# Three changes of order in a gated Fourier and attention kernel: half of q earlier, the gate earlier, a first chunk in pieces

## The chip, the cores and the metric

The kernel runs on one core of a Trainium2 chip. The metric is the device time of one execution in microseconds (us). A core has TensorE (PE in the profile; its weight loads are PEld), VectorE (DVE), ScalarE (ACT), GpSimd (POOL) and SyncE (SP), which only issues transfers. Each engine works through its own list of instructions in order and waits on semaphores for the others. Transfers are issued mostly from SyncE's queue, some from POOL's, and are carried out by 16 DMA engines.

## The reference

For x of 2048 rows and 512 columns the output mixes two branches with one gate per row:

```python
g = _sigmoid((x * gate_w).sum(-1, keepdims=True))
# branch a: real part of a Fourier transform along both axes, as matrix products
a = einsum("bsd,ed->bse", x, dft_hid_re);  b = einsum("bsd,ed->bse", x, dft_hid_im)
y = einsum("ts,bse->bte", dft_seq_re, a) - einsum("ts,bse->bte", dft_seq_im, b)
# branch b: attention with 32 heads of width 16
q, k, v = split(x @ wqkv)                       # per head: 2048 x 16
p = softmax(einsum("bhqd,bhkd->bhqk", q, k) * Dh ** -0.5)
o = einsum("bhqk,bhkd->bhqd", p, v) @ wo
return g * y + (1 - g) * o
```

All of it is float32.

## The kernel before, in words

Nearly every float32 factor is cut into a rounded high part and a low part (`hi_lo`: ACT copies to the high part, DVE or POOL subtracts to get the low part), and a product is made of three matrix products: high times high, high times low, low times high (`mm3`).

*Stage 1, q and k (lines 132 to 199).* x (four blocks of 512 rows, each in four chunks of 128 columns) and the weights of q, k and v are loaded as raw tiles of 128 x 512 into `RAW` = 6 buffers. `add` puts a load on a list; `load_ahead` (L113) issues loads from the list as long as fewer than five loaded tiles are waiting; `split(n)` (L118) cuts the next n of them into parts and loads on. The list starts with chunk 0 of q's weights and of x, then chunk 1 of both, and so on. TensorE first does ten products with zeros (L161), then `split(8)` has cut the first four chunks, and the products of the first chunk come in the order: four times weights high with x high, four times weights low with x high, four times weights high with x low (L183); then the other chunks with `mm3` (L91 to L93). Results go out as high and low parts to `qk_d` in memory. For the last two blocks of x `gate_row` (L166) sums x times gate_w on DVE into a column of `z`.

*Stage 2, v (L358 to L365).* After `qs` and `ks` were cleared, v is made: four chains of 12 products (L362), then three times `four` (L333), which runs four chains in half-height products with some of the attention's row maxima in between.

*Stage 3, imaginary hidden transform (L375), then `run_plan(0)`, the gate (`gate`, L764 to L770: one exponential on ACT, four operations on 128 x 16 elements on DVE, giving `g`, `ng` and `omg`), and a `four` with the weights `wre` (L1046).* `g` is used from the first results of the sequence transform on, `ng` and `omg` later.

*Stage 4, the long stage.* Two heads make a pair p (0 to 15). A pair is 32 units: for each half of the queries (columns LOW, 0 to 1023, and HIGH) 16 key tiles. Per unit the scores are computed (`scores`, L788) from `ks[p % 2]` and `qs[p % 2]`, ACT takes the exponential (L789), and `pv` (L824) multiplies with v. Before that, `a_tile` (L248) computes scores the other way round, and DVE reduces them to row maxima (L250); these maxima, negated, become three extra rows of `qs`, so that the scores come out already reduced. The sequence transform of branch a runs through the same segments (L457).

A segment is written out as a pattern of slots:

```python
FULL = "s a s s a a s s a a s a s a a s |"
```

In each slot one product of the transform runs on one half of the rows of the array, and beside it on the other half a score (s) or a maximum (a) of one head: head 1 in even segments, head 0 in odd ones. At the bar come late work, the sums, `run_plan(valued)`, and then the value products of two units. So a segment takes two units, and eight scores and eight maxima of one head.

*What sets the order of the loads.* `at(u, f, ...)` puts a call into a plan; `run_plan(u)` makes all calls that are due by u + 1. For pair p, with u = 32(p - 1), `load_q(p, LOW)` is put at u - 14, the loads of `ks` in quarters at u - 16 (head 1) and u - 14 (head 0) and every four units after that, `load_q(p, HIGH)` at u - 2. `load_q` (L227) issues three transfers from `qk_d` (L220) and one of zeros (`clear`, L225) that empties the rows of the maxima. On SyncE's queue there are also the stores of `osum` (L842, a half pair's result, which wait for POOL's sum), the chunks of `w_seq` (`c_load`, L392, one for every 12 products of the transform), the loads and stores of the normalising blocks (`block`, L582 to L602), and the rows of maxima (`m_rows`, L271, half of them on POOL's queue). Pairs alternate between `qs[0]` and `qs[1]`, so the load for pair p overwrites columns that the scores of pair p - 2 read: LOW is read by units 32(p - 2) to 32(p - 2) + 15, that is up to u - 17.

Of the kernel before, what the change touches and what calls it, by code (L numbers as in the profile page):

```python
# [10 lines left out]
F32 = mybir.dt.float32  # L11
F32R = mybir.dt.float32r
AF = mybir.ActivationFunctionType
ALU = mybir.AluOpType
AX = mybir.AxisListType

P = 128
# [5 lines left out]
KT = D // P  # L23
# [3 lines left out]
RAW = 6  # L27
# [5 lines left out]
def mix_kernel(ctx: ExitStack, tc: tile.TileContext, xa_t, xa, wqkv, w_hid, w_seq, wo, gate_w, out):  # L33
# [5 lines left out]
    nc = tc.nc  # L39
# [26 lines left out]
    z = const.tile([P, NT], F32, name="z")  # L66
    g = const.tile([P, NT], F32, name="g")
    ng = const.tile([P, NT], F32, name="ng")
    omg = const.tile([P, NT], F32, name="omg")
# [5 lines left out]
    xab = [const.tile([P, 4, 2, D], F32R, name=f"xab{tb}", tag=f"xab{tb}") for tb in range(4)]  # L75
# [10 lines left out]
    def hi_lo(hi, lo, src, lo_eng=None):  # L86
        nc.scalar.copy(hi, src)
        (lo_eng or nc.vector).tensor_tensor(lo, src, hi.bitcast(F32), ALU.subtract)

    def mm3(ps, sh, sl, mh, ml, first, last):  # L90
        nc.tensor.matmul(ps, sh, mh, start=first, stop=False)  # L91
        nc.tensor.matmul(ps, sh, ml, start=False, stop=False)  # L92
        nc.tensor.matmul(ps, sl, mh, start=False, stop=last)  # L93
# [9 lines left out]
    todo, loaded = [], []  # L103

    def staged(src):
        raw = st1.tile([P, D], F32, name="raw", bufs=RAW)
        nc.sync.dma_start(raw, src)
        return raw

    def add(hi, lo, src, lo_eng, shape=None):  # L110
        todo.append((hi, lo, src, lo_eng, shape))

    def load_ahead():  # L113
        while todo and len(loaded) < RAW - 1:
            hi, lo, src, lo_eng, shape = todo.pop(0)
            loaded.append((hi, lo, staged(src), lo_eng, shape))

    def split(n):  # L118

        for _ in range(n):  # L120
            load_ahead()
            if loaded:
                hi, lo, raw, lo_eng, shape = loaded.pop(0)
                hi_lo(hi, lo, raw.rearrange("p (s t) -> p s t", s=4) if shape else raw, lo_eng)
            load_ahead()

    def add_x(tb, kt):
        x = xab[tb][:, :, :, kt * P:(kt + 1) * P]
        add(x[:, :, 0], x[:, :, 1], xa_t[tb, :, kt], nc.vector, True)


    with tc.tile_pool(name="qk", bufs=1, reuse_waits="tile") as pool:
        wh = pool.tile([P, 2, KT, D], F32R, name="wh")
        wl = pool.tile([P, 2, KT, D], F32R, name="wl")

        def mm_qk(ps, c, ct, tb, kt):
            cols = slice(ct * P, (ct + 1) * P)
            x = xab[tb][:, :, :, kt * P:(kt + 1) * P]
            mm3(ps, wh[:, c, kt, cols], wl[:, c, kt, cols], x[:, :, 0], x[:, :, 1], kt == 0, kt == KT - 1)

        def evac_qk(ps, c, ct, tb):
            hl = pool.tile([P, 2, D], F32R, name="hl", bufs=7)
            hi_lo(hl[:, 0], hl[:, 1], ps)
            nc.sync.dma_start(qk_d[c][:, ct * P:(ct + 1) * P, tb * 512:(tb + 1) * 512].rearrange("v p t -> p v t"),
                              hl.bitcast(F32))

        for kt in range(KT):
            add(wh[:, 0, kt], wl[:, 0, kt], wqkv[0, :, kt], nc.vector)
            add_x(0, kt)
        for kt in range(KT):  # L150
            add(wh[:, 1, kt], wl[:, 1, kt], wqkv[1, :, kt], nc.vector)
        for tb in range(1, 4):
            for kt in range(KT):
                add_x(tb, kt)
        for kt in range(KT):
            add(wv[0][kt], wv[1][kt], wqkv[2, :, kt], nc.gpsimd)
        for kt in range(KT):
            add(wch[:, kt], wcl[:, kt], w_hid[1, :, kt], nc.gpsimd)
        ps = turn_of("f")
        for _ in range(10):  # L160
            nc.tensor.matmul(ps, zero, zero.unsqueeze(1).broadcast_to([P, 4, P]), start=True, stop=True)  # L161
        split(8)

        xgs = {}

        def gate_row(s):  # L166

            xg = xgs.pop(s)
            nc.vector.scalar_tensor_tensor(xg, xg, 1.0, gwb, op0=ALU.mult, op1=ALU.mult, accum_out=z[:, s:s + 1])
            if s + 5 < NT:  # L170
                xgs[s + 5] = staged(xa[s + 5])

        for tb in range(4):
            if tb == 2:
                assert not todo and not loaded
                nc.sync.dma_start(gwb, gate_w.broadcast_to([P, D]))
                xgs.update({s: staged(xa[s]) for s in range(5)})
            for c in range(2):
                if tb == 0 and c == 0:
                    pss = [turn_of("f") for _ in range(4)]  # L180
                    for w, v in ((wh, 0), (wl, 0), (wh, 1)):
                        for ct in range(4):
                            nc.tensor.matmul(pss[ct], w[:, c, 0, ct * P:(ct + 1) * P], xab[tb][:, :, v, :P],  # L183
                                             start=w is wh and not v, stop=False)
                    for kt in range(1, KT):
                        for ct in range(4):
                            mm_qk(pss[ct], c, ct, tb, kt)
                    split(4)
                    for ct in range(4):
                        evac_qk(pss[ct], c, ct, tb)  # L190
                    continue
                for ct in range(4):
                    ps = turn_of("f")
                    for kt in range(KT):
                        mm_qk(ps, c, ct, tb, kt)
                    split(1 if ct % 2 and tb else 2)
                    evac_qk(ps, c, ct, tb)
                    if tb > 1:
                        gate_row(8 * (tb - 2) + 4 * c + ct)
# [32 lines left out]
    LOW, HIGH = slice(0, S // 2), slice(S // 2, S)  # L232
# [93 lines left out]
    def maxima():  # L326

        nonlocal a_next
        users = [a_tile(a_next, h) for h in range(2)]
        a_next += 1  # L330
        return users[1]

    def four(ss, wh, wl, done, between=None):  # L333

        ps = [turn_of("s") for _ in ss]
        seen = None
        for phase, pair in enumerate(((0, 1), (2, 3), (1, 0), (3, 2))):
            guard, seen = seen, None
            both = [row_products(ss[c], wh, wl) for c in pair]
            for j in range(12):  # L340
                for half, c in enumerate(pair):
                    st, mv = next(both[half])
                    r = slice(64 * half, 64 * half + 64)
                    i = nc.tensor.matmul(ps[c], st[r], mv[r], start=phase < 2 and j == 0, stop=phase > 1 and j == 11)  # L344
                    if phase > 1 and j == 0:
                        tc.add_manual_dep(
                            i.ins, guard.ins.name,
                            mybir.DependencyInfo(mybir.DependencyClass.Sync, mybir.DependencyReason.DATA))
                if j in (((2, 7), (1, 5, 10), (3, 8), (1, 5, 10))[phase] if not between else (2, 6, 10)):
                    user = between(phase, j) if between else maxima()  # L350
                    seen = seen or user
            if deferred:
                deferred.pop(0)()
            if phase > 1:
                for c in sorted(pair):
                    done(ss[c], ps[c])

    for s in range(4):  # L358
        ps = turn_of("s")
# [401 lines left out]
        x.products((0,))  # L761


    def gate():  # L764

        nc.scalar.activation(ng, z, AF.Exp, bias=0.0, scale=-1.0)
        nc.vector.tensor_scalar(ng, ng, 1.0, None, op0=ALU.add)
        nc.vector.reciprocal(g, ng)
        nc.vector.tensor_scalar(ng, g, -1.0, None, op0=ALU.mult)
        nc.vector.tensor_scalar(omg, g, -1.0, 1.0, op0=ALU.mult, op1=ALU.add)  # L770

    pts = {}

    def scores(u, qb, h, ps=None):
# [109 lines left out]
    def at(u, f, *args):  # L884
        plan.setdefault(u, []).append(partial(f, *args))

    for p in range(2, NP):
        u = 32 * (p - 1)
        at(u - 14, load_q, p, LOW)
        for kb in range(4):  # L890
            cols = slice(kb * 512, (kb + 1) * 512)
            if 2 < p < NP - 1:
                at(u - 16 + 4 * kb, load_rows, p, 1, cols, (1,))
                at(u - 14 + 4 * kb, load_rows, p, 1, cols, (0,))
            else:
                at(u - 14 + 4 * kb, load_rows, p, 1, cols)
        at(u - 2, load_q, p, HIGH)

    for hf in range(2):
        for ct in range(4):  # L900
            n = 3 if hf and ct == 3 else 4
# [119 lines left out]

    both_first = chain_of(proj(1, (0, 1, 2), one), proj(0, (0, 1, 2), one))
    run_plan(0)
    gate()

    first_y = []

# [76 lines left out]
```

## Time and profile before

| | us |
|---|---|
| median of 3 runs | 1681.37 |
| lowest and highest | 1680.41, 1682.21 |
| the profiled execution | 1678.57 |
| its span, first to last instruction | 1676.4 |
| TensorE busy in it | 1659.6 (99%) |
| VectorE busy | 1375.9 (82%) |
| ScalarE busy | 1252.2 (75%) |
| GpSimd busy | 753.5 (45%) |

The granted TensorE clock was 0.999 over the span. Lines of the profile are quoted below as they stand. A row of the timeline is: start, duration, engine, line, operation, out<-in, shapes, count, and in brackets the idle time of the engine before it with what ended it. A row of the waits is: who waited, for whom, microseconds in total, times, the longest. A row of the chain is: start, duration, what ran. "SPq" is SyncE's queue issuing a transfer. L12 is line 12 of the kernel.

### The profile page before, as it was taken

Reading aid. Unit: us, or ns where it says so; the run is one execution under the profiler, and the core shown is the slowest. Engines: PE = TensorE matmul, PEld = TensorE weight load, DVE = VectorE, ACT = ScalarE, POOL = GpSimd, SP = SyncE. Lnnn points to the kernel's source line nnn. Section 1 sums busy time; section 2 is a strip of 40 time slices with the busy share of each in tenths; the row PEclk is TensorE's granted clock in tenths of the full one; section 3 lists DMA queues with packets and bytes.
Section 4 is the critical chain, followed back from the end, with each engine's and each line's share of the span. In section 5 each row is a group of like instructions: output and inputs, shape, how many; then the busy total and the mean of one; then the engine's idle time right before and its main releaser. Section 6 shows DMA issues by size and latency. Waiting matters only on the chain.

```text
span 1676.4 us, 35226 instructions
## 1 busy us (share of the span) xinstructions
PE 1659.6 (99%) x13170; PEld 991.0 (59%) x13170; DVE 1375.9 (82%) x2283; ACT 1252.2 (75%) x2486; POOL 753.5 (45%) x813
## 2 busy tenths in 40 slices
PE   9999999999999999999999999999999999999998
PEld 7888866655555555555555555555555555555554
DVE  5469988888888888888888888888888888877775
ACT  5212288878777787777787777877778788799996
POOL 0124644445454455544454555555445565432331
PEclk9999999999999999999999999999999999999999
DMA  9944301112121224222127324222222234451014
GB/s 299 341 152 142 155 1 38 28 55 77 55 72 47 69 83 123 73 58 71 50 79 245 85 89 124 85 82 73 65 71 64 80 96 124 157 189 47 15 53 140
DMA packets 92481, 165.66 MB, mean 99 GB/s; under 512 B 23360, under 2 KB 24776, under 8 KB 91160
## 3 DMA queue, kind: packets, MB, share of 16 engines
q1 hardware_dynamic: 87672, 162.64, 31.3%
q8 instruction: 104, 1.70, 0.4%
q0 software_dynamic: 4352, 0.39, 0.2%
q14 instruction: 65, 0.53, 0.1%
q10 hardware_dynamic: 288, 0.39, 0.1%
HBM read 107.73 MB, written 54.52 MB: 97 GB/s over the span
## 4 chain that ended last, share of the span: by engine, by line
PE 97%; DMA 1%; DVE 1%; SPq 1%; ACT 0%; issue 0%; DVEq 0%; ACTq 0%
PE d L457 36%; PE t L824 27%; PE t L248 11%; PE t L788 10%; PE t L344 5%; PE t L92 2%; PE t L93 2%; PE t L91 2%; PE t L805 1%; PE t L457 1%; PE t L362 1%; PE d L248 0%; SPq L220 0%; DMA ks<-qk 0%; DVE mx L250 0%; DMA qs<-zero 0%
## 5 line engine op out<-in xcount | busy, mean ns | idle before, releaser
L250 DVE TENSOR_REDUCE mx<-t 128x1 f32<-128x512 f32 x2009 | 1251.7, 684 | 230.4 <-PE t L248 198.9
L789 ACT ACTIVATE pt<-t 128x512 f32<-128x512 f32 x2048 | 1034.8, 632 | 19.8 <-PE t L788 9.5
L788 PE MATMUL t<-qs,ks 64*128 64x512 f32 x2048 | 728.4, 409 | 0.2
L248 PE MATMUL t<-ks,qs 64*128 64x512 f32 x2009 | 674.1, 398 | 8.6 <-DMA qs<-zero 3.6
L457 PE MATMUL d<-xab,ch 64*128 64x512 f32 x2016 | 657.1, 400 | 0.0
L824 PE MATMUL t<-pt,vt 128*32 128x512 f32 x3968 | 477.1, 598 | 0.0
L457 PEld LDWEIGHTS d<-xab,ch 64*128 64x128 f32 x2016 | 359.2, 184 | 142.4 <-issue 97.3
L248 PEld LDWEIGHTS t<-ks,qs 64*128 64x128 f32 x2009 | 358.5, 184 | 85.4 <-ACT pt L789 50.5
L788 PEld LDWEIGHTS t<-qs,ks 64*128 64x128 f32 x2048 | 366.6, 184 | 69.6 <-DVE mx L250 40.0
L457 PE MATMUL d<-xab,cl 64*128 64x512 f32 x1008 | 404.0, 401 | 0.0
L839 POOL TENSOR_TENSOR osum<-osum,oe 128x512 f32<-128x512 f32 x217 | 279.5, 1288 | 157.9 <-ACT oe L833 155.3
L833 ACT COPY oe<-t 128x512 f32<-128x512 f32 x217 | 127.4, 587 | 214.8 <-PE t L824 213.1
L824 PEld LDWEIGHTS t<-pt,vt 128*32 128x32 f32 x3968 | 103.6, 109 | 232.1 <-issue 150.5
L402 POOL CAST ch<-craw 128x512 fp32r<-128x512 f32 x126 | 77.2, 613 | 359.6 <-PE t L788 290.3
L457 PEld LDWEIGHTS d<-xab,cl 64*128 64x128 f32 x1008 | 185.7, 184 | 72.7 <-issue 50.3
L403 POOL TENSOR_TENSOR cl<-craw,ch 128x512 fp32r<-128x512 f32 x126 | 162.3, 1288 | 10.2
L271 POOL DMA_DIRECT2D qs<-mt x132 | 73.6, 563 | 88.7 <-DVE mt L267 78.8
L457 PE MATMUL d<-wo_hl,o_hl 64*128 64x512 f32 x288 | 75.8, 395 | 0.0
L457 PE MATMUL d<-wre,xab 64*128 64x512 f32 x288 | 70.4, 389 | 0.0
L457 PEld LDWEIGHTS d<-wo_hl,o_hl 64*128 64x128 f32 x288 | 51.6, 184 | 18.3 <-ACT pt L789 13.4
L457 PEld LDWEIGHTS d<-wre,xab 64*128 64x128 f32 x288 | 52.8, 184 | 3.1
L92 PE MATMUL t<-xab,wh 128*128 128x512 f32 x124 | 48.3, 389 | 0.0
(118 smaller groups left out, 944.8 us busy)
## 6 DMA issues: line engine op xcount, KB each, us to landing
craw<-w_seq SPq DMA_DIRECT2D x128, 256.0 KB
qk<-hl SPq DMA_DIRECT2D x32, 512.0 KB
qs<-qk SPq DMA_DIRECT2D x84, 128.0 KB
ks<-qk SPq DMA_DIRECT2D x288, 32.0 KB
b<-hl SPq DMA_DIRECT2D x16, 512.0 KB
xab<-b SPq DMA_DIRECT2D x16, 512.0 KB
o<-osum SPq DMA_DIRECT2D x62, 128.0 KB
oh<-nh SPq DMA_DIRECT2D x12, 512.0 KB
```

The lines of the kernel that those rows point to most:

```text
L92: nc.tensor.matmul(ps, sh, ml, start=False, stop=False)
L248: nc.tensor.matmul(ps, qs[p % 2][r, qt * P:(qt + 1) * P], ks[p % 2][r, kb * 512:(kb + 1) * 512], start=True, stop=True)
L250: user = nc.vector.tensor_reduce(mx[p % 2][:, h, qt, kb:kb + 1], ps, AX.X, ALU.max)
L344: i = nc.tensor.matmul(ps[c], st[r], mv[r], start=phase < 2 and j == 0, stop=phase > 1 and j == 11)
L402: nc.gpsimd.tensor_copy(h1, raw)
L403: nc.gpsimd.tensor_tensor(l1, raw, h1.bitcast(F32), ALU.subtract)
L457: i = nc.tensor.matmul(self.ps, st[r], mv[r], start=not self.begun, stop=stop)
L788: nc.tensor.matmul(ps, ks[p % 2][rr, kt * P:(kt + 1) * P], qs[p % 2][rr, q0:q0 + 512], start=True, stop=True)
L789: return nc.scalar.activation(pts[u][:, 2 * qb + h], ps, AF.Exp, bias=0.0, scale=DH ** -0.5)
L824: nc.tensor.matmul(acc[32 * j:32 * j + 32], vt[:, kt, p, h:h + 32], pt[:, j], start=u == us[0], stop=u == us[-1])
L833: nc.scalar.copy(oe, acc)
L839: nc.gpsimd.tensor_tensor(o, o, oe, ALU.add)
```

## The change

Three things are moved. First, `load_q(p, LOW)` is planned at u - 18 in place of u - 14, for all pairs from 2 on. Second, the five operations of the gate stand ahead of the chains of v in place of behind `run_plan(0)`. Third, the first chunk: x is loaded first and its weights second, outside of the list; x's high part is made first on ACT; the high part of the weights is made in four pieces of 128 columns, alternately on DVE and ACT; then DVE makes the low part of the weights and that of x. Nine products with zeros are done in place of ten, and `split(6)` follows for the other three chunks. No arithmetic is added or left out beside the one product with zeros.

```diff
-    def load_ahead():
-        while todo and len(loaded) < RAW - 1:
+    def load_ahead(n=RAW - 1):
+        while todo and len(loaded) < n:
...
-        for kt in range(KT):
+        first = staged(xa_t[0, :, 0]), staged(wqkv[0, :, 0])
+        for kt in range(1, KT):
             add(wh[:, 0, kt], wl[:, 0, kt], wqkv[0, :, kt], nc.vector)
             add_x(0, kt)
...
-        for _ in range(10):
+        for _ in range(9):
             nc.tensor.matmul(ps, zero, zero.unsqueeze(1).broadcast_to([P, 4, P]), start=True, stop=True)
-        split(8)
+        load_ahead(RAW - 2)
+        x, raw = xab[0][:, :, :, :P], first[0].rearrange("p (s t) -> p s t", s=4)
+        nc.scalar.copy(x[:, :, 0], raw)
+        for ct in range(4):
+            cols = slice(ct * P, (ct + 1) * P)
+            (nc.scalar.copy if ct % 2 else nc.vector.tensor_copy)(wh[:, 0, 0, cols], first[1][:, cols])
+        nc.vector.tensor_tensor(wl[:, 0, 0], first[1], wh[:, 0, 0].bitcast(F32), ALU.subtract)
+        nc.vector.tensor_tensor(x[:, :, 1], raw, x[:, :, 0].bitcast(F32), ALU.subtract)
+        split(6)
...
+    nc.scalar.activation(ng, z, AF.Exp, bias=0.0, scale=-1.0)
+    nc.vector.tensor_scalar(ng, ng, 1.0, None, op0=ALU.add)
+    nc.vector.reciprocal(g, ng)
+    nc.vector.tensor_scalar(ng, g, -1.0, None, op0=ALU.mult)
+    nc.vector.tensor_scalar(omg, g, -1.0, 1.0, op0=ALU.mult, op1=ALU.add)
+
     for s in range(4):
         ps = turn_of("s")
...
-        at(u - 14, load_q, p, LOW)
+        at(u - 18, load_q, p, LOW)
...
     run_plan(0)
-    gate()
```

More of the change, by code (lines that the diff above doesn't have):

```diff
@@ L761, in last_pair @@
         x.products((0,))
[L764 to L770, printed above, removed]
     pts = {}
```

## The prediction

> **What bounds the kernel now.** I read the page first. The chain of work that ended last is almost all matrix products, so only time in which TensorE stands still, or is held to a slower pace, can be won or lost.
>
> ```profile
> PE 97%; DMA 1%; DVE 1%; SPq 1%; ACT 0%; issue 0%; DVEq 0%; ACTq 0%
> ```
>
> Next the view of waits for TensorE alone. Its idle time in the whole span is small, and nearly all of it stands in front of L248, the products of `a_tile`:
>
> ```profile
> PE t L248 <- DMA qs<-zero: 3.6, 2, 2.9
> PE t L248 <- DMA ks<-qk: 3.4, 2, 1.7
> PE t L248 <- ACT pt L789: 1.3, 2, 1.0
> ```
>
> Then the chain in order of time. Every group of value products (L824, 16 products) marks the end of one segment of the plan, so the distance between two groups is one segment. The list leaves some groups out; a distance of two segments is then split.
>
> ```profile
> 356.42 1.85 PE t L824 x16
> 362.73 1.85 PE t L824 x16
> 368.54 1.85 PE t L824 x16
> ...
> 449.89 1.85 PE t L824 x16
> ...
> 457.58 1.85 PE t L824 x16
> ...
> 544.68 1.85 PE t L824 x16
> 550.67 1.85 PE t L824 x16
> ...
> 631.92 1.86 PE t L824 x16
> 642.84 2.80 DMA qs<-zero
> ...
> 646.75 1.85 PE t L824 x16
> ...
> 733.82 1.85 PE t L824 x16
> ...
> 741.61 1.86 PE t L824 x16
> ...
> 916.05 1.85 PE t L824 x16
> ...
> 928.50 1.85 PE t L824 x16
> ...
> 1015.53 1.90 PE t L824 x16
> ...
> 1022.58 1.85 PE t L824 x16
> ```
>
> A regular segment takes 368.54 - 362.73 = 5.81 us. Once in each pair of heads a segment is longer. Pair 3: 362.73 - 356.42 = 6.31, an excess of 0.50. Pair 4: 7.69, excess 1.88. Pair 5: 5.99, excess 0.18. Pair 6: 646.75 - 631.92 = 14.83 for two, excess 3.21. Pair 7: 7.79, excess 1.98. Pair 9: 928.50 - 916.05 = 12.45 for two, excess 0.83. Pair 10: 7.05, excess 1.24. Together 9.82 us. It is always the segment that ends at unit u - 12 of its pair (u = 32(p - 1)), and by the pattern FULL its 14th slot of 16 holds the first `a_tile` of pair p, for head 1. That product is the first reader of the LOW columns of `qs`, which `load_q` writes at u - 14: three transfers of q and one of zeros.
>
> SyncE's queue shows why they are late (pair 6, then pairs 9 and 5):
>
> ```profile
> 627.83 0.38 SPq L392 DMA_DIRECT2D craw<-w_seq  x1
> ...
> 634.62 1.15 SPq L842 DMA_DIRECT2D o<-osum  x2
> ...
> 640.90 1.76 SPq L220 DMA_DIRECT2D qs<-qk  x3
> ```
>
> ```profile
> 920.64 1.78 SPq L220 DMA_DIRECT2D ks<-qk  x3
> ```
>
> ```profile
> 542.26 1.74 SPq L220 DMA_DIRECT2D qs<-qk  x3
> ```
>
> One issue takes about 0.6 us of the queue. In pair 6 the two stores of `osum` had waited, and the loads of `ks`, the four loads of a normalising block and a chunk of `w_seq` stood ahead of q. So q went out at 640.90 and the zeros at 642.84, the product began at 645.77 by the chain (642.84 + 2.80, and the wait's tail), 2.9 us late. In pair 5 q went out at 542.26, ahead of its segment (which begins with the group at 544.68), and the excess is only 0.18. I read the excess as lateness of q plus about 0.18 us that the first products on freshly written columns cost anyway.
>
> **The change part by part.**
>
> *First half of q four units sooner.* Nothing is added or removed: the same four issues go onto SyncE's queue two segments (11.6 us) earlier in program order, for pairs 2 to 15. In pair 6 that is after the load at 627.83, where the queue did little until the stores at 634.62. The four take 640.90 to 643.50 = 2.6 us there. What they are moved past: the stores of `osum`, three loads of `ks` for head 1 (u - 16), block loads and one or two chunk loads. Those now start up to 2.6 us later if the queue is full, and not at all later where it stood waiting for POOL's sum, as in pair 6. The loads of `ks` for head 0, behind q at u - 14, go 2.6 us sooner. What the moved loads must wait for: they overwrite columns that the scores of pair p - 2 read, units up to u - 17. FULL gives eight scores of one head to a segment, that is four units; by the plan at u - 18 head 1 has all of unit u - 17 from the segment before, and head 0 has reached u - 15. So the last reader runs in the first half of the segment that precedes the plan, and the queue does not stand long. Both q and zeros should then have landed some 5 us or more before the first reader.
>
> What is late next is `ks` of head 1. In pair 9 its issue ends at 920.64 + 1.78 = 922.42. In pair 6 the reader started 645.77 - 643.50 = 2.3 us after the last issue ended, so `ks` can be read at 924.7. The reader is due 5.1 us after its segment's first group (pair 6: 645.77 less the wait of 2.9 is 642.9, the group is at 631.92 + 5.81 = 637.7), in pair 9 at 916.05 + 5.81 + 5.1 = 927.0. That leaves 2.3 us, so the cover holds in the worst pair that I found.
>
> Worth: 9.82 us less seven times the 0.18 that pair 5 keeps, 9.82 - 1.26 = 8.6 us. Ends: 5 us if `ks` or a slow transfer takes back some of the places, 11 us if nothing at all remains and the pairs that I have not listed give another half microsecond each. I take 8.6, from the rows of pair 5.
>
> *The gate ahead of the v chains.* One exponential on ACT and four small operations on DVE move from the start of the stage with `wre` to the start of the v chains.
>
> ```profile
> 198.79 0.75 DVE L767 TENSOR_SCALAR ng<-ng 128x16 f32<-128x16 f32 x1 [0.24 <-ACT ng L766]
> ```
>
> ```profile
> 199.35 1.09 PE L344 MATMUL t<-wre,xab 64*128 64x512 f32 x8
> ...
> 200.82 1.41 PE L344 MATMUL t<-wre,xab 64*128 64x512 f32 x8
> ...
> 204.47 1.30 PE L344 MATMUL t<-wre,xab 64*128 64x512 f32 x8
> ...
> 205.61 1.29 PE L344 MATMUL t<-wre,xab 64*128 64x512 f32 x8
> ```
>
> Before, DVE is held by the gate between its maxima, and TensorE waits for the banks that those maxima free. Groups of eight products (with two products for maxima between them) come every 205.61 - 204.47 = 1.14 us; behind the gate the distance is 200.82 - 199.35 = 1.47, so 0.33 us too long. In the new place the work is covered: DVE has nothing there.
>
> ```profile
> 105.05 2.08 DVE L250 TENSOR_REDUCE mx<-t 128x1 f32<-128x512 f32 x3 [7.95 <-PE t L248]
> ```
>
> The added wait, ACT's for the last row of `z`, has the copies of `v` behind it, and these wait longer for other things; if the cover were gone the price would be the gate's own length, some 1.5 us. Ends: a gain of 1.5 us (all of the gate) and a loss of 1.5; I take a gain of 0.3, the rows' figure.
>
> *The first chunk.* x is loaded and copied first, the weights are copied in four pieces on DVE and ACT, and one of ten warming products goes.
>
> ```profile
> 1.06 4.63 PE L161 MATMUL t<-zero 128*128 128x512 f32 x10 [1.06 <-DVE zero L60]
> ...
> 4.91 0.62 ACT L87 CAST xab<-raw 128x512 fp32r<-128x512 f32 x1 [0.23 <-DMA raw<-xa_t]
> ...
> 5.58 1.23 PE L183 MATMUL t<-xab,wh 128*128 128x512 f32 x4
> ...
> 7.17 0.62 ACT L87 CAST xab<-raw 128x512 fp32r<-128x512 f32 x1 [0.36 <-DMA raw<-xa_t]
> ...
> 7.82 0.69 DVE L88 TENSOR_TENSOR xab<-raw,xab 128x512 fp32r<-128x512 f32 x1 [0.29 <-ACT xab L87]
> ...
> 8.70 0.40 PE L92 MATMUL t<-xab,wh 128*128 128x512 f32 x1
> ...
> 12.10 1.29 ACT L87 CAST wh<-raw 128x512 fp32r<-128x512 f32 x2 [1.64 <-DMA raw<-wqkv]
> ```
>
> The second transfer lands at 4.91 in either order. A quarter of a 0.62 us copy is about 0.2 us, so the first product may start near 5.2 in place of 5.58: 0.4 us at most. But the second chunk's x lands at 7.17, its low part is ready at 7.82 + 0.69 = 8.51, and the product that needs it ran at 8.70. It can move up by 0.13 us only; that is what I take. The seventh load now waits for the low part of the first x, about 1.4 us later than before (behind two more operations of 0.69 us on DVE). The loads behind it may shift as much, and the first weights of k, copied at 12.10, with them to 13.5, their low part to about 14.9. TensorE wants them after its first 48 products, which at 0.23 us each end at 5.58 + 11.0 = 16.6: covered. Ends: a gain of 0.4 and a loss of 1.4 (that delay uncovered).
>
> Sum: 8.6 + 0.3 + 0.1 = 9.0 us. The profiled execution took 1678.57 us, so it would take 1669.6. It lies 2.8 us under the median shown, 1681.37, which would become 1672.4.
>
> **The rivals.**
>
> *The places are taken by `ks` or by a slow transfer.* Pair 10 speaks for it. There q went out together with its segment's first group:
>
> ```profile
> 1015.46 1.77 SPq L220 DMA_DIRECT2D qs<-qk  x3
> ```
>
> With the zeros behind it, its issue ended 2.6 us later at 1018.1, and by pair 6's 2.3 us it could be read at 1020.4, when the reader was due (1015.53 + 5.1 = 1020.6). The segment still had 1.24 us too much; the wait is put down to ACT. I think that the transfer was slow. The profile's queues include fetches of instructions:
>
> ```profile
> q8 instruction: 104, 1.70, 0.4%
> ```
>
> 1.70 MB in 104 packets is 16 KB a packet, and one in the way could hold up a transfer of q or `ks`. [...] If four pairs in twelve pay 1.24 us for `ks`, the gain is 9.0 - 5.0 = 4.0: 1677.4 us. Against: by the working above `ks` has 2.3 us to spare even in pair 9.
>
> [...]
>
> *The regained time is given back.* If DVE and ACT had used the pauses to catch up, the same time would be lost in the following segments: 1681 us. Against: the segment behind pair 3's long one takes the regular 5.81, so nobody ran ahead in the pause.
>
> *Slower: SyncE's queue stands at the moved load.* If the load at u - 18 could go only when scores much later than u - 17 were done, everything behind it would stand as well, the stores, `ks` of head 1, the chunks. The queue has 634.62 - 628.21 = 6.4 us to spare in pair 6, of which the moved issues take 2.6, and the reader of `ks` has 2.3 us (pair 9): up to 6.1 us of standing are free. Each further microsecond costs twelve, one in each of the pairs 3 to 14, so from 6.1 + 9.0 / 12 = 6.9 us on the change loses; at 8 us it would be 23 us less the 9.0 won: 1695 us. Against: in pair 5 q went out at 542.26, while the second half of pair 3 was still being scored, so the wait is for columns and not for the tile.
>
> **How the numbers follow.** About 0.2%, 3.4 us, can be told from no change here. Chances: the forecast 0.75 (its own range 1668.5 to 1674.5, gains of 7 to 13), `ks` or slow transfers 0.09, the clock 0.03, given back 0.06, slower 0.07. The low end allows for both ends of q and gate and for longer pauses in the unprofiled runs; the high end takes in the first two rivals: 1668.0 to 1677.5. Faster 0.87, same 0.06, slower 0.07.
>
> **What would show it.** Right: the view of waits has no row of L248 behind `qs<-zero`; the segments that end at u - 12 are 5.8 to 6.0 us; q goes out some 10 us ahead of its segment; no gate operation at 198 us, and groups of 1.14 us there; the product at 8.70 some 0.1 us sooner. Wrong: waits of L248 on `ks<-qk` of the old size, waits of SyncE on products at L220 of many microseconds, or segments over 5.81 throughout.

## The result, and the profile after

| | before, us | changed, us |
|---|---|---|
| median of the runs | 1680.89 (4 runs, 1680.25 to 1682.21) | 1668.14 (4 runs, 1668.07 to 1668.79) |
| the profiled execution | 1678.57 | 1668.08 |
| its span | 1676.4 | 1666.0 |

The ratio is 0.9924, 95% interval 0.9907 to 0.9941. The change wins 12.75 us by the medians and 10.5 us by the two profiled executions. Forecast were 9.0 us, 1672.4; the result lies just inside the low end of the range (1668.0), and 0.4 us under the forecast's own range of 1668.5 to 1674.5. So two questions stand: did the gain come by the steps that were named, and where do the further 3.75 us come from?

The view of waits for TensorE, changed kernel. Nothing of L248 (now L257) is left in it; the first row is the start of the program:

```profile
PE t L162 <- DVE zero L60: 1.1, 1, 1.1
PE t L192 <- DVE wh L168: 0.2, 1, 0.2
```

The chain in order of time, changed kernel; the groups of value products are L831 here. Two rows stand for each of the pairs 4, 6, 7, 9 and 10; what was the long segment ends with the second.

```profile
448.75 1.85 PE t L831 x16
454.62 1.85 PE t L831 x16
...
634.65 1.85 PE t L831 x16
640.53 1.85 PE t L831 x16
...
727.59 1.85 PE t L831 x16
733.47 1.86 PE t L831 x16
...
913.63 1.85 PE t L831 x16
919.50 1.85 PE t L831 x16
...
1006.64 1.85 PE t L831 x16
1012.57 1.85 PE t L831 x16
```

They take 5.87, 5.88, 5.88, 5.87 and 5.93 us where a regular one takes 5.81. Over pairs 3 to 14 the excess fell from 10.97 to 0.95 us, so 10.0 us of the profiled difference is here.

SyncE's queue around pair 6, changed kernel: q and zeros go out between the chunk load and the stores, from 625.25, 7.6 us ahead of `ks` of head 1.

```profile
624.78 0.38 SPq L407 DMA_DIRECT2D craw<-w_seq  x1
625.25 1.78 SPq L229 DMA_DIRECT2D qs<-qk  x3
627.21 0.64 SPq L234 DMA_DIRECT2D qs<-zero  x1
630.38 0.59 SPq L617 DMA_DIRECT2D oh<-nh  x1
631.62 1.15 SPq L849 DMA_DIRECT2D o<-osum  x2
632.87 1.81 SPq L229 DMA_DIRECT2D ks<-qk  x3
```

The stage with `wre`, timeline of TensorE, changed kernel: the groups of eight follow at 1.14 and 1.13 us, and the gate stands on DVE at 96.87.

```profile
199.23 1.07 PE L353 MATMUL t<-wre,xab 64*128 64x512 f32 x8
...
200.37 1.07 PE L353 MATMUL t<-wre,xab 64*128 64x512 f32 x8
...
201.50 1.07 PE L353 MATMUL t<-wre,xab 64*128 64x512 f32 x8
```

```profile
96.87 0.11 DVE L368 TENSOR_SCALAR ng<-ng 128x16 f32<-128x16 f32 x1
```

From the first product with `wre` to the first value products it is 18.76 us in place of 19.47, so 0.7 us. Over all fourteen profiles of this case the figure is 18.76 to 18.88 with the gate moved and 19.38 to 19.47 without. The start, timeline of the changed kernel: the product that ran at 8.70 runs at 8.61.

```profile
4.34 0.62 ACT L165 CAST xab<-raw 128x512 fp32r<-128x512 f32 x1 [2.32 <-DMA raw<-xa_t]
...
5.42 1.31 PE L192 MATMUL t<-xab,wh 128*128 128x512 f32 x4 [0.15 <-DVE wh L168]
...
8.61 0.39 PE L92 MATMUL t<-xab,wh 128*128 128x512 f32 x1
```

The tail from the last value products to the end is 0.25 us longer (13.40 against 13.15).

### The profile page after: what moved, and what is told of

Same layout as the page of the kernel before. It is cut to its first block, busy times and chain, and to the rows that moved or that the text cites. A ratio compares the mean times of both kernels' runs of the same rounds, so it can differ in the third digit from the quotient of the medians.

```text
span 1666.0 us, 35235 instructions
## 1 busy us (share of the span) xinstructions
PE 1657.4 (99%) x13169; PEld 986.3 (59%) x13169; DVE 1374.9 (83%) x2285; ACT 1251.8 (75%) x2487; POOL 753.6 (45%) x813
## 4 chain that ended last, share of the span: by engine, by line
PE 99%; DVE 0%; DMA 0%; DVEq 0%; SPq 0%; issue 0%
PE d L472 38%; PE t L831 28%; PE t L257 11%; PE t L795 9%; PE t L353 5%; PE t L93 2%; PE t L91 2%; PE t L92 2%; PE t L812 1%; PE t L472 1%; PE t L377 1%; DVE mx L259 0%; DMA raw<-wqkv 0%; PE t L192 0%; DVE yp L664 0%; PE t L749 0%
## 5 line engine op out<-in xcount | busy, mean ns | idle before, releaser
L257 PE MATMUL t<-ks,qs 64*128 64x512 f32 x2009 | 672.7, 398 | 0.1
L831 PE MATMUL t<-pt,vt 128*32 128x512 f32 x3968 | 477.1, 598 | 0.0
L257 PEld LDWEIGHTS t<-ks,qs 64*128 64x128 f32 x2009 | 358.4, 184 | 75.7 <-ACT pt L796 43.9
L831 PEld LDWEIGHTS t<-pt,vt 128*32 128x32 f32 x3968 | 103.6, 109 | 231.9 <-issue 148.9
```

The lines of the kernel that those rows point to most:

```text
L257: nc.tensor.matmul(ps, qs[p % 2][r, qt * P:(qt + 1) * P], ks[p % 2][r, kb * 512:(kb + 1) * 512], start=True, stop=True)
L831: nc.tensor.matmul(acc[32 * j:32 * j + 32], vt[:, kt, p, h:h + 32], pt[:, j], start=u == us[0], stop=u == us[-1])
```

## The experiments

The kernel before ran beside each set; its medians there were 1679.44 (29 runs), 1680.26 (15) and 1679.89 (15), with single runs from 1677.7 to 1683.9. Times of the first four experiments go against the first, of the next four against the second, of the last four against the third.

**Each part alone, and the kernel before again.**

```diff
q_only (of the kernel before)
-        at(u - 14, load_q, p, LOW)
+        at(u - 18, load_q, p, LOW)
```

> Only the load of q's LOW half moves to u - 18; gate and first chunk as before. My theory: the gain is the pauses of TensorE ahead of the first product on fresh columns of qs, so nearly all of the change's 12.7 us is here: about 11.9 us faster (1669.0), and no wait of TensorE on qs<-zero in the profile. If only the pauses that the profiled execution of before showed were won (the segments that end at u - 12 were 10.1 us longer in sum than after), 10 us (1671). Rival: gate and first chunk bring the rest that the profile does not explain, then 9 to 10 us here.

Measured: 1668.55 us, ratio 0.9934 (0.9922 to 0.9947), 10.9 us faster. The excess of the twelve long segments is 0.97 us, as in the whole change, and no wait of TensorE on `qs<-zero` is left. Nearly all of the gain is this one line. The time lies between the theory's 11.9 us and the 10 us of the pauses in the first profile; the interval, 8.9 to 13.1 us, holds both, and the rival's 9 to 10 us too, so this time alone does not tell them apart.

```diff
gate_only (of the kernel before): the five operations of gate() moved
+    nc.scalar.activation(ng, z, AF.Exp, bias=0.0, scale=-1.0)
...
     for s in range(4):
         ps = turn_of("s")
...
     run_plan(0)
-    gate()
```

> Only the gate moves ahead of the v chains. Theory: 0.7 us faster, the difference of the two profiles between the start of the stage with wre and the first value products (19.47 to 18.76 us). Rival: the gate accounts for the 2 us that the profiles leave unexplained: 2.5 to 3 us faster.

Measured: 1679.40 us, ratio 1.0002 (0.9992 to 1.0011): no difference in the time can be told. The profile shows the gain in its place (18.88 us from `wre` to the first value products, against 19.43 in the run of the kernel before below), and its tail is 13.17. The runs of a kernel with the pauses spread too far to show half a microsecond. The rival's 2.5 us is excluded: the interval reaches to 1.3 us.

```diff
chunk_only (of the kernel changed): q back to u - 14, the gate back behind run_plan(0)
-        at(u - 18, load_q, p, LOW)
+        at(u - 14, load_q, p, LOW)
```

> Only the first chunk is changed (x first, pieces, nine warming products). Theory: 0.1 us faster, too little to be told from no change; in the profile the stage of v begins 0.1 us sooner. Rival: 2 us faster in unprofiled runs, because the clock is released sooner or the loads stand better.

Measured: 1678.68 us, ratio 0.9994 (0.9985 to 1.0003): not told from no change. Across the profiles the stage of v begins at 92.70 to 93.26 us with the new first chunk and at 92.79 to 93.30 with the old one; 0.1 us drowns in that. The rival's 2 us is not excluded by this run, whose interval reaches to 2.5 us; beside a kernel without pauses it is (q_gate below).

> The kernel before, unchanged, as a run of its own. Theory: same time, but the long segments (those that end at u - 12) differ in sum by 1 us or more from the first profile, because the pauses hang on when transfers land; runs spread over some 2 us. Rival: the same long segments to a tenth of a microsecond in every execution; then the 2.3 us between the profiled execution and the median of before lie elsewhere.

Measured: 1679.71 us, ratio 1.0001 (0.9993 to 1.0010). The long segments' excesses are not the same in the two executions: pair 3 has 0.99 in place of 0.50, pair 6 3.66 in place of 3.23, pair 9 1.70 in place of 0.84, pair 10 0.06 in place of 1.24. In sum they differ by 0.2 us only, so the 1 us of the theory is missed; and the runs spread over 5 us, not 2. And something appeared that the first profile did not have. The chain in order of time, run of the kernel before:

```profile
632.16 1.86 PE t L824 x16
643.13 2.52 DMA qs<-zero
647.43 2.74 PE t L824 x16
654.13 1.85 PE t L824 x16
659.91 1.85 PE t L824 x16
```

Behind the pause the value products take 2.74 us in place of 1.85, and the next segment 654.13 - 647.43 = 6.70 us in place of 5.81. Busy time by stretches, same run, then the first profile of before. A row is: the stretch, its length, the busy time of PE, PEld, DVE, ACT and POOL with their instructions, the granted clock, the DMA share and GB/s:

```profile
642.00:646.00 4.00, 1.27 (x12) 0.78 (x10) 2.29 (x4) 1.96 (x5) 1.26 (x1) 0.97 0.57 183
646.00:650.00 4.00, 4.00 (x22) 1.24 (x22) 1.29 (x2) 0.60 (x1) 0.00 (x0) 0.60 0.10 28
650.00:654.00 4.00, 4.00 (x36) 2.98 (x32) 3.11 (x6) 3.70 (x8) 1.81 (x2) 1.00 0.35 86
```

```profile
646.00:650.00 4.00, 4.00 (x34) 1.95 (x34) 1.99 (x4) 1.87 (x4) 0.00 (x0) 1.00 0.14 37
```

The granted clock is 0.60 in the mean of the 4 us behind the pause, and TensorE does 22 products where it did 34 in the other execution. The same stands behind pair 6 in gate_only and q_back, and behind the shorter pause of pair 4 in chunk_only:

```profile
458.00:462.00 4.00, 4.00 (x21) 1.27 (x22) 0.85 (x2) 1.21 (x3) 0.00 (x0) 0.57 0.28 77
```

So a pause can cost more than its length: about 0.9 us in the segment behind it in before_again and gate_only, 0.7 us in q_back, 1.6 us in chunk_only. Of the six profiles with q at u - 14 and once issued zeros (before_filled below among them) five show such a drop, and the first one, on which the prediction rested, is the one without. None of the seven with q earlier shows it.

The trace's own records of the clock are sharper than means over 4 us. Each drop in them goes to 0.50 and lasts 3.41 us, or 6.83, and the edges of one execution lie on one grid of 3.41 us. Stretches cut on that grid, around pair 6 in before_again and in the first profile of before, and around pair 4 in chunk_only:

```profile
642.38:645.79 3.41, 0.68 (x8) 0.22 (x4) 1.91 (x4) 1.58 (x4) 1.26 (x1) 1.00 0.57 189
645.79:649.21 3.42, 3.42 (x18) 1.40 (x22) 1.29 (x2) 0.60 (x1) 0.00 (x0) 0.50 0.11 34
```

```profile
640.59:644.01 3.42, 2.23 (x20) 1.46 (x16) 3.41 (x6) 3.12 (x7) 2.31 (x2) 1.00 0.83 250
644.01:647.42 3.41, 1.65 (x14) 0.84 (x18) 1.20 (x3) 0.60 (x1) 0.00 (x0) 1.00 0.15 47
```

```profile
455.02:458.43 3.41, 1.55 (x16) 0.72 (x18) 2.28 (x5) 1.43 (x4) 0.00 (x0) 1.00 0.28 77
458.43:461.84 3.41, 3.41 (x20) 1.02 (x14) 0.42 (x1) 0.82 (x2) 0.00 (x0) 0.50 0.27 72
```

In before_again nearly the whole pause lies in one stretch, in which TensorE is busy for 0.68 us, and the clock is halved in the next. In the first profile the pause is no shorter (2.9 us against 2.7), but the edge at 644.01 cuts it: TensorE is busy for 2.23 and 1.65 us in the two stretches, and the clock stays. Over all fourteen profiles the records show 28 drops, half of them at the end of the program; each follows a stretch of which TensorE was busy for 0.456 or less, and of the other 6792 stretches at full clock none lies under 0.474. So it is the share of the pause that falls into one stretch that goes with the drop, and the same kernel drops in one execution and not in another.

The place of the grid differs between executions (edges at 642.38 and 645.79 in before_again, at 640.59 and 644.01 in the first profile of before). A pause of 1.9 us was enough for a drop in pair 4 of chunk_only, with TensorE busy for 1.55 us of the stretch. What sets the grid and the half no run shows.

**Half the distance.**

```diff
q16 (of the kernel changed)
-        at(u - 18, load_q, p, LOW)
+        at(u - 16, load_q, p, LOW)
```

> The changed kernel, but with q's LOW half at u - 16, ahead of the loads of ks for head 1 on SyncE's queue. Theory: q is early enough, but ks of head 1 now goes out 2.6 us later and has 2.3 us to spare in pair 9 by the prediction's working, so pair 9 shows a pause of some 0.4 us and perhaps pair 6 a little; all else as in the changed kernel: 1668.1 to 1669. Rival: lateness is not decided by the queue's order but by the two segments of distance; then about half of the pauses come back, 1673 to 1675.

Measured: 1669.73 us, ratio 0.9937 (0.9925 to 0.9950). The pauses are gone, as my theory had it, so one segment is enough; as the run moves q ahead of `ks` and by a segment at once, it does not tell which of the two counts. The 0.4 us in pair 9 did not come: `ks` went out there at 915.60 to 917.38, two microseconds ahead of its reader, and that was enough. In its place each of the twelve segments has an excess of 0.14 to 0.21 us, 2.07 in sum in place of 0.95.

**A transfer more in front.**

```diff
clear3 (of the kernel before, in load_q)
-            clear(qs[p % 2], slice(3, P, 32), cols)
+            for _ in range(1 if cols == HIGH else 3):
+                clear(qs[p % 2], slice(3, P, 32), cols)
```

> The kernel before with the transfer of zeros into the LOW half issued three times in place of once, so that the last of the four to six transfers goes out some 1.5 us later; the values are the same. Theory: each pair that waited already waits 1.5 us more (pairs 3, 4, 6, 7, 9, 10, 12, 14: eight), the early ones (5, 8, 11, 13) do not: 12 us slower, 1693. Rival: the transfers' landing is set by the bytes in front of them and not by the queue's issues; then 2 us slower at most.

Measured: 1744.50 us, ratio 1.0382 (1.0368 to 1.0396): 64 us slower, five times what I expected. The expectation took an issue's length for the price. But each of the repeated transfers writes what the one before wrote, and the queue waited for its own transfers, 28 times and 46.4 us in all. SyncE's waits and the timeline of its queue in pair 6:

```profile
SPq L225 <- DMA qs<-zero: 46.4, 28, 1.9
```

```profile
661.30 5.43 SPq L225 DMA_DIRECT2D qs<-zero  x3
```

And behind the pauses, now 7.3 us in pair 6, the clock fell. The records show a drop behind each of the nine pauses of 3.9 to 7.3 us, seven of them for 6.83 us and two for 3.41 us:

```profile
662.00:668.00 6.00, 0.00 (x0) 0.00 (x0) 0.49 (x1) 0.15 (x1) 0.17 (x1) 0.78 0.14 36
668.00:672.00 4.00, 3.47 (x18) 1.47 (x22) 1.29 (x2) 0.60 (x1) 0.00 (x0) 0.50 0.12 33
```

The long segments' excess is 59.9 us, and some 15 us more were lost outside of them than in the kernel before's profiles, most of it in the segments behind the drops. The four pairs that I took to be early enough (5, 8, 11, 13) waited too, 0.6 to 4.0 us. The run supports the chain from a late transfer to a pause; its size can't tell the queue's issue time from anything, because the edit made a wait of its own.

**What is late next.**

```diff
ks_late (of the kernel changed)
-                at(u - 16 + 4 * kb, load_rows, p, 1, cols, (1,))
+                at(u - (16 if kb else 14) + 4 * kb, load_rows, p, 1, cols, (1,))
```

> The changed kernel, but with the first quarter of ks for head 1 at u - 14 in place of u - 16, so that it goes out about where q went before (one set of three issues and not four, with nothing of q in front). Theory: ks of head 1 is what is late next; its last issue ends about 1.8 us after the segment's first group in quiet pairs (in time for a reader due 5.1 us after it) and 2 to 5 us after it where blocks and chunks stand ahead (pairs 4, 6, 7, 10, 12, 14), so pauses of 0.5 to 2 us come back there: 1671 to 1675, with waits of TensorE on ks<-qk. Rival: ks never decides; no difference, 1668.1.

Measured: 1669.45 us, ratio 0.9936 (0.9923 to 0.9950). Pauses come back in pairs 4 (0.70), 7 (0.62) and 6 (0.36), three of the six that I named, and smaller: 1.3 us over the changed kernel's 1668.14, which ran in another set, where I expected 3 to 7. TensorE's waits:

```profile
PE t L257 <- ACT pt L796: 0.5, 1, 0.5
PE t L257 <- DMA ks<-qk: 0.4, 1, 0.4
```

So `ks` of head 1 is what is late next, one segment behind its place in the changed kernel.

**Gate and first chunk together.** q_back is the changed kernel with q at u - 14, the edit of q_only the other way round.

> The changed kernel with q's LOW half back at u - 14: gate and first chunk together. Theory: the gains of the two parts add up, 0.8 us faster than the kernel before (1680.1), and the long segments are back. Rival: the parts hang together, and 2 to 3 us of the gain stay.

Measured: 1678.21 us, ratio 0.9993 (0.9984 to 1.0002): the long segments are back (11.6 us of excess), and 0.8 us can't be told from nothing here. That 2 to 3 us stay isn't excluded by the medians, 2.05 us apart, but the interval reaches from -2.7 to +0.3 us.

**The pauses filled with work.**

```diff
before_filled (of the kernel before), after_filled (of the kernel changed), in a_tile
+        if h == 1 and i % 64 == 0:
+            for _ in range({4: 6, 6: 10, 7: 6}.get(p, 0)):
+                nc.tensor.matmul(ps, zero, zero.unsqueeze(1).broadcast_to([P, 4, P]), start=True, stop=True)
```

> The kernel before, with 6, 10 and 6 products with zeros (0.23 us each, into a bank whose next product overwrites them) ahead of the first product on fresh q in pairs 4, 6 and 7: 5.0 us of added work laid into the three pauses of some 1.9, 3.2 and 1.9 us. Theory: the pauses cost more than their length because TensorE's granted clock falls to about 0.6 behind some of them; with the pauses filled the clock stays at 1.00, so that in spite of the added work it is 1 to 2.5 us faster than before, with less spread. Rival: only the length of the pauses counts and the filler hides in it: same as before within 0.2%. Second rival: the filler lengthens the pauses: 1 to 5 us slower.

> The changed kernel with the same 22 products with zeros. There are no pauses to lay them into: 5.0 us slower than the changed kernel, 1673.1. If it is less, the changed kernel still has idle time at these places.

Measured: before_filled 1682.29 us, ratio 1.0013 (1.0004 to 1.0022), so 2.4 us slower and not faster. after_filled 1674.67, 6.5 us slower than the changed kernel beside it (1668.19), not 5.0. Both missed. The second rival's figure for before_filled came true, but not by its reason, as the profile shows below. The 22 products cost more than I took: in the profile of after_filled the three segments that hold them have an excess of 1.78, 2.71 and 1.76 us, 6.0 us more than in the changed kernel. In the profile of before_filled the filler lies in the pauses, which are no longer for it (excess 2.04, 3.05, 2.04 in place of 1.88, 3.23, 1.98), and behind them the clock stays up. But pair 9, which has no filler, waited 3.2 us there, and the clock fell behind it:

```profile
PE t L251 <- DMA qs<-zero: 3.9, 3, 3.2
```

```profile
930.00:934.00 4.00, 3.46 (x18) 1.46 (x22) 1.29 (x2) 0.60 (x1) 0.00 (x0) 0.50 0.14 33
934.00:938.00 4.00, 4.00 (x28) 1.92 (x22) 1.08 (x2) 2.03 (x4) 0.00 (x0) 0.66 0.35 90
```

In after_filled too, pair 9 has 1.7 us of excess without any filler, with a wait on `ks` that the changed kernel does not have:

```profile
PE t L260 <- DMA ks<-qk: 1.5, 1, 1.5
```

In both, the transfer was late because SyncE's queue was: q went out 3.9 us behind its segment's first group in before_filled (926.07 against 922.15; 1.4 us in the first profile of before), and `ks` 2.4 us behind it in after_filled (921.97 against 919.56; in the changed kernel both are at 913.63). In both a packet of 16 KB of an instruction fetch ran in a place where the queue's issues took longer than elsewhere: from 923.26 to 924.94, where three issues of `ks` took 3.43 us in place of 1.8, and from 906.59 to 907.91, where two loads of `xab` took 1.85 us in place of 0.82. I take the added products to have moved such fetches to worse places; it was not tested by a run of its own.

What the filler shows is that the pauses hid some 6 us of work. It did not save the clock over the runs: of the eleven runs of before_filled one has a granted clock of 0.999, seven have 0.998 and three 0.997, no better than the fifteen of before beside them (five, seven, and three from 0.995 to 0.997).

**Without the new first chunk.** q_gate joins the edits of q_only and gate_only; after_again is the changed kernel.

> Load of q and gate changed, first chunk as before. Theory: 0.5 us faster than with q alone (the gate's 0.7 less the few tenths by which the end of the kernel was longer in the profiles that have gate and first chunk together), 1667.9 to 1668.1, so as fast as the whole change or 0.1 us faster. Rival: the first chunk is worth 0.1 to 0.4 us and this is slower than the whole change, 1668.3 to 1668.5.

> The changed kernel once more, beside the other three: 1668.1, with a spread below 1 us.

Measured: q_gate 1668.15 us, ratio 0.9929 (0.9916 to 0.9941); after_again 1668.19 us, ratio 0.9930 (0.9916 to 0.9944), five runs each, from 1667.98 to 1668.93 together. The new first chunk brings nothing that can be measured. The profiles agree with the theory in one point: the tail is 13.17 us in q_gate and 13.39 in after_again. It is 0.2 us longer in every profile that has gate and first chunk together and in none that has one of them; why is open. q_gate and the changed kernel can't be told apart, and no version beat them.

## Why the prediction was right

*What bounds the kernel, and the step of q.* Right. The excess of the segments that end at u - 12 was lateness of q, and the one line takes it away (q_only). Three of the waits that the prediction showed seem to speak against it, two put down to `ks` (pairs 4 and 7, 3.4 us) and one to ACT (pair 10). The trace's semaphore records answer them; a transfer of q or `ks` lands there in 16 parts. When the product of pair 4 started, at 456.62, the `ks` transfer named, issued at 454.71, had landed in 8 of its 16 parts, so the product can't have waited for it; the zeros had landed at 456.38. In pair 7 it was 13 of 16 at 740.66, with the zeros there at 740.41. In pair 10 fifteen parts of the last q transfer had landed by 1019.63 and the sixteenth came at 1021.48, 0.14 us ahead of the product. So it was q or its zeros in all three.

The price per pair was read too low in two terms. The residue: I took 0.18 us from pair 5, and the changed kernel keeps 0.06 to 0.12, 0.95 us over twelve pairs, so that 10.0 us and not 8.6 were won by the profile. I had also left five pairs out of the list, worth 0.7 us of that.

*The further gain.* The forecast was 3.75 us short. The two profiles explain 1.5 us of that: 1.4 us more from the long segments, 0.4 us more from the gate, 0.25 us less for the longer tail. The other 2.25 us stand between the profiled execution of before and the median of its four runs, 1680.89. Some 1 us of them is that these four runs lay high beside the later ones: the 59 runs of before in the three sets have a median of 1679.89. The rest is a term that was missing: the drop of the granted clock behind a pause. I had given the clock a chance of 0.03, with the start of the program in mind, and held the pauses for worth their length. The profile of before that I had was the one execution of six that shows no drop; I noted that it was faster than the median, and put it aside.

The lists of runs, with the granted clock of each, fit this. Of the 59 runs of before 21 have 0.999 and a median of 1678.49 us, 29 have 0.998 and 1679.98, nine have 0.995 to 0.997 and 1682.10; one drop of 3.41 us to half is 0.001 of the span. Of the nine runs of the changed kernel eight have 0.999. So the runs of before with the highest clock stand within 0.1 us of the profiled execution and 10.3 us above the changed kernel, nearly what the two profiles show, and the 1.4 us from there to the median of all 59 go with a lower clock. That the changed kernel's runs lie within 0.7 us of each other where those of before spread over 6 fits too. It is not shown that the drops alone cost the 1.4 us: the pauses change from execution to execution as well (pair 9's excess is between 0.6 and 1.7 us), and a drop stood behind each of clear3's nine pauses of 3.9 to 7.3 us, but behind those of 1.9 to 3.2 us in some executions only.

*The gate.* Right in place and sign: forecast 0.3 us, measured 0.7 in the profile, 0.6 in gate_only's. I had counted one distance of two groups; the whole stage ran steadily afterwards. In the time it shows only beside a kernel without pauses: q_gate is 0.4 us under q_only, though the two ran in different sets.

*The first chunk.* Forecast 0.1 us, 0.09 in the profile (8.70 to 8.61), and no difference in time. The bound that I named, x of the second chunk, did not set the end in the profiled execution: its low part was ready at 8.28, while the weights landed later than I took (copied from 5.04, not 4.91) and the first product started at 5.42, not 5.2.

*The rivals.* `ks` in q's place: not in the changed kernel, but ks_late shows that it is next, and the slow transfer that I suspected in pair 10 is borne out by its sixteenth part, which came 1.85 us behind the others; a fetch packet of 16 KB ran from 1019.15 to 1020.08, but that it held the part up is not shown. The clock, at 0.03: that a product with zeros fewer, or a pause behind them, makes the slow start longer no run shows. By the trace's records products start 0.43 us apart from 1.65 up to 5.06 in the kernel before and 0.23 apart from 5.97; in the changed kernel, with one product fewer and 0.15 us of idle time behind them, it is up to 4.64 and from 5.87. The high end of the range does not hang on it, as `ks` alone gives 1677.4. The regained time was not given back. SyncE's queue stood at the moved load in pair 9 only, where the four issues took from 905.19 to 910.47 in place of 2.6 us, and nothing came of it. The free time that I read for this rival in pair 6 was too long: a store of `oh` went out at 633.38, so 5.2 us and not 6.4 were free ahead of it, and 4.9 us of standing, not 6.1. My figure for the slack of `ks`, 2.3 us after the issue's end, came from the zeros, which landed later than `ks` (in the first profile of before 1.76 us after the end of their issue in the median, 2.13 in pair 6, and `ks` 1.54, in pair 6 1.44 for the last of head 1); q16 shows that two microseconds were enough.

## What to carry to other kernels

Look for long segments that come back at a fixed place in the loop, and follow the transfer that ends them back through the queue that issues it: what stands in front of it there decides, and moving it forward to where the queue stood idle, with the readers of the old data through, cost nothing here (q_only is 10.9 us faster). Compare the profiled execution with the other runs, and their granted clocks with each other: one profile is one execution, and here the first was the one of six without a drop, so profile the kernel again before pricing a wait. A pause of TensorE of two to three microseconds was worth its length here and, in executions where it left TensorE busy for 0.456 or less of one stretch of 3.41 us, 0.7 to 1.6 us more (before_again, gate_only, q_back, chunk_only).

## What was not expected of the hardware

The granted clock fell to 0.50 behind pauses of 1.9 us (pair 4 of chunk_only) to 3.2 us (pair 9 of before_filled), for 3.41 or 6.83 us, in some executions and not in others. A drop came when TensorE had been busy for 0.456 or less of one stretch of 3.41 us, and none at 0.474 or more.

A product that must wait for many transfers seems to cost time here even when all have landed (in pairs 5, 8 and 11 of q16 at least 1.9 us before). By the trace's records of semaphores, over twelve profiles and without the segments that had real pauses, the excess of the segment is 0.18 us on average where the first two products on new columns wait for seven semaphores (29 segments), 0.08 where for five (56), and 0.06 where for three or fewer (18). That may be 1.1 of the 1.6 us by which q16, with no pauses, was still slower than the changed kernel. No run was made for it alone.

Three transfers of the same zeros to the same place took 5.43 us of the queue where one takes 0.66: the queue stood 46 us in all for transfers that it had issued itself.
